# The diagonal ahead of the next chunk's first product, the ranks half a step later, and half of the row-rest moves on SyncE

## The chip, the cores and the metric

The kernel runs on one core of a Trainium2 chip. The metric is the time of one execution on the device in microseconds, the median over several runs. Engines are named as in the profile: PE is TensorE's matrix unit, DVE VectorE, ACT ScalarE, POOL GpSimd, and SP is SyncE, which here issues transfers (DMAs) and does no arithmetic.

## The reference

Three layers, one after another. An attention layer with a running state is computed for 4 x 8 heads over 768 tokens; its output becomes 3072 rows of 384, which go through a gated layer and then through a layer of 8 experts, of which each row takes one.

```python
state = np.zeros((B, H, D, D))
for t in range(S):
    kt, vt, rt = k[:, :, t], v[:, :, t], r[:, :, t]
    cur = np.einsum('bhd,bhe->bhde', u[None] * kt, vt)
    y[:, :, t] = np.einsum('bhd,bhde->bhe', rt, state + cur)
    state = w[None, :, :, None] * state + np.einsum('bhd,bhe->bhde', kt, vt)
x = y.transpose(0, 2, 1, 3).reshape(B * S, H * D)
x = ((1 / (1 + np.exp(-(x @ w_gate)))) * (x @ w_val)) @ w_out
logits = normalized(x) @ normalized(expert_emb).T / tau
e = argmax(logits, axis=1)
out = softmax(logits)[e] * (np.maximum(x @ w1[e], 0) @ w2[e])
```

## The kernel before, in words

The tokens are cut into 24 chunks of 128 (six to a batch). A chunk's inputs come in one load of 1152 KB (`load_chunk`) into a tile `ld`, of which there are two buffers, or `ldr`, a third one for every third chunk (2, 5, 8 and on). `load_chunk(c + 3)` stands at the end of chunk c, so a load waits until the chunk three before has been used up.

What is done with a chunk c is cut into stages:

- `at_p` (stage -2): products that scale the loaded fields. From chunk 9 on POOL does all five: rT by its table (L540), kT by its table (L541), r by k (L542), r by u (L543), k by its table (L544). Before chunk 9 one product on DVE (L538) does the first two.
- `at_s1` (stage 1): DVE sums the r products to `sd` (L552), and `at_diag` writes the diagonal of the score tile `Am` from it, on POOL (L564; up to chunk 5 partly on ACT).
- stage 2, `native_mask`: the scores that PE has left in PSUM are copied into `Am` above the diagonal by two predicated copies on DVE (L591).
- stage 4 (`at_P`, `at_Y1`, `at_T`), stage 5 (`at_Y2` and the next chunk's scores, `native_A`) and stage 6 (`at_X`, `at_D`, `load_chunk(c + 3)`). All of them put PE products into two PSUM banks, named `a0` and `a1` by their tags (tiles `py`). `at_X` writes the chunk's output, split in two words, to `xt`, and for the fourth part of the dims to `xp3`; `at_D` moves that part with six small transfers of 32 KB each for two chunks (L688) into the last 16 of each 64 rows of `xt`. All six are issued by POOL.

The gated layer runs over groups g of two chunks; from group 2 on two groups together, in steps of a gate half (`pgate`, nine products of 128x512, then ACT's sigmoid), a value half (`pval`, nine, then DVE's product `sgw`, ACT's `gth`, DVE's `gtl`) and twelve products into `o`. `at_tick` is called after each half, so a half step is the unit in which chunk stages are dealt out between these products. When a group's last `o` is there, `route_pick` chooses the expert of each row; two ticks later `route_rank` counts the rows per expert: three small PE products into `pr` (L782 to L784), which takes the bank `a1`, then four small DVE operations (L786 to L791), then POOL scatters the rows to DRAM (L793, `xs`).

`at_tick` calls the chunk stages of the tick first and then, if no chunk is between its stages 4 and 2 of the next (`open_y` is empty), the ranks that are due. So a rank that fell due beside a stage 2 stood directly behind the mask in the program. `pr` and the scores that the mask reads share bank `a1`, so `pr` waits until the mask has been read out.

After the groups come the experts, whose weights are loaded and split while PE multiplies. The library orders instructions of one engine by its own estimate of when each is ready, unless `follow(ins, before)` pins two of them.

Of the kernel before, what the change touches and what calls it, by code (L numbers as in the profile page):

```python
# [8 lines left out]
F32 = mybir.dt.float32  # L9
# [28 lines left out]
EARLY = 9  # L38
# [21 lines left out]
def kernel(  # L60
# [14 lines left out]
    nc = tc.nc  # L75
# [223 lines left out]
    if True:  # L299
# [45 lines left out]
        wd = c1.tile([P, 4], F32, name="wd")  # L345
        nc.sync.dma_start(out=wd, in_=wdec)
        ld = {}

        def load_chunk(c):
            if c % 3 == 2:  # L350
                t = r2p.tile([P, 3072], F32, tag="r2", name="ldr")[:, 0:2304]
            else:
                t = ldp.tile([P, 2304], F32, tag="ld", name="ld")
            for a, b in ((0, 1024), (1024, 2304)) if c == 0 else ((0, 2304),):
                nc.sync.dma_start(out=t[:, a:b], in_=att[c][:, a:b])
            ld[c] = t

        load_chunk(0)
# [147 lines left out]
        xp3 = c1.tile([P, 2, 256], F32R, name="xp3")  # L506
# [23 lines left out]

        def at_p(c):
            rT, kT, kt, v, r = fields(ld[c])
            if c < EARLY:

                nc.gpsimd.tensor_tensor(r, r, kt, op=ALU.mult)
                nc.gpsimd.tensor_tensor(r, r, ubt, op=ALU.mult)
                rk = ld[c][:, 0:1024].rearrange("p (b a n) -> p b a n", b=2, a=4)
                nc.vector.tensor_tensor(rk, rk, tabs, op=ALU.mult)  # L538
            else:
                nc.gpsimd.tensor_tensor(rT, rT, tabR, op=ALU.mult)  # L540
                nc.gpsimd.tensor_tensor(kT, kT, tabK, op=ALU.mult)  # L541
                nc.gpsimd.tensor_tensor(r, r, kt, op=ALU.mult)  # L542
                nc.gpsimd.tensor_tensor(r, r, ubt, op=ALU.mult)  # L543
            nc.gpsimd.tensor_tensor(kt, kt, tabKt, op=ALU.mult)  # L544
# [11 lines left out]
        def at_diag(c):  # L556
            if c < 4 and c % 2 == 1:
                Am = xtp.tile([P, 3072], F32, tag="xt", name="Am1")[:, 0:512].rearrange("p (h n) -> p h n", h=8)
            else:
                Am = Am0  # L560
            ams[c] = Am
            n = ACT_HEADS[c] if c < len(ACT_HEADS) else 0
            if n < 8:
                nc.gpsimd.tensor_tensor(  # L564
                    Am[:, n:8], same.unsqueeze(1).to_broadcast([P, 8 - n, HALF]),
                    sd[c % 2][:, n:8].unsqueeze(2).to_broadcast([P, 8 - n, HALF]), op=ALU.mult,
                )
            for h in range(n):
                nc.scalar.activation(Am[:, h, :], same, AF.Copy, scale=sd[c % 2][:, h:h + 1])

# [112 lines left out]
        def at_D(c):  # L683
            x = xt[c // 4][:, :, :, (c % 4 - 1) * P:(c % 4 + 1) * P]
            if c % 2 == 1 and c >= PERM:
                for h in range(2):
                    for k in range(3):
                        nc.gpsimd.dma_start(  # L688
                            out=x[64 * h + 48:64 * h + 64, k], in_=xp3[64 * h + 16 * k:64 * h + 16 * k + 16]
                        )  # L690

        gts = {}
        last_lo = []
        po = {}
        open_y = []
        scores = {}
# [287 lines left out]
        def rank_due(n):  # L984
            for r in ranks:
                r[0] -= 1
            while ranks and ranks[0][0] <= n:
                route_rank(*ranks.pop(0)[1])
# [114 lines left out]
        tick = 0  # L1103

        def at_tick():
            for c, st in sorted(stages.get(tick, [])):
                at_stage(c, st)
            if not open_y:
                rank_due(0)

        for g, f, wide in steps:
            if wide == 2:
# [366 lines left out]
```

## Time and profile before

| | |
|---|---|
| median of 3 runs | 851.79 us (848.81 to 854.65) |
| profiled execution | 849.21 us, span of its instructions 847.4 us |
| PE busy | 807.7 us, 95% of the span |
| DVE, ACT, POOL busy | 411.9, 321.8 and 243.7 us |
| granted TensorE clock, mean | 0.979 of full speed |
| POOL's small moves (L688) | 60 instructions, 31.1 us |

PE is busy in nine tenths or more of nearly every fortieth of the span; the exceptions are the first, a few slices around 120 to 160 us, two near 280 and 375 us, and the end. Idle time on the other engines costs nothing by itself. A wait is put down to what came last before the waiting instruction could start. Times of rows are microseconds from the start of the span.

### The profile page before, as it was taken

What the parts mean: (1) busy time and instruction counts of PE and PEld (TensorE: products, weight loads), DVE (VectorE), ACT (ScalarE), POOL (GpSimd) and SP (SyncE); (2) the same over time, 40 slices, a digit from 0 to 9 for tenths busy, and PEclk for the clock granted to TensorE, in tenths of its full rate; (3) what the DMA queues carried; (4) which work ended last, traced back from release to release, by engine and by line L of the source; (5) the groups of instructions that cost most, each with busy time, mean ns of one, the idle gap of its engine ahead of it and who ended that gap; (6) DMA issues with size and microseconds to landing.
All of it is one profiled execution on the core that took longest, in us unless ns stands there. A gap on an engine that the chain in (4) does not pass through costs nothing.

```text
span 847.4 us, 16892 instructions
## 1 busy us (share of the span) xinstructions
PE 807.7 (95%) x6941; PEld 722.2 (85%) x6941; DVE 411.9 (49%) x912; ACT 321.8 (38%) x695; POOL 243.7 (29%) x298
## 2 busy tenths in 40 slices
PE   5999998899999899979999999999999999999994
PEld 4889998788888788868878888888999989899993
DVE  6998764533343333433443324434474555565630
ACT  4776733222232122312232224334454455465530
POOL 6621034843435434453433111100210110110211
PEclk8699999999999999999999999999999999999997
DMA  8667832331212112121211002520476556554301
GB/s 325 262 237 276 264 105 76 123 105 58 66 57 84 35 53 64 73 83 56 67 57 31 21 10 71 182 74 0 109 241 203 171 189 212 170 194 141 122 20 34
DMA packets 36003, 100.03 MB, mean 118 GB/s; under 512 B 4731, under 2 KB 19207, under 8 KB 32975
## 3 DMA queue, kind: packets, MB, share of 16 engines
q1 hardware_dynamic: 29311, 87.27, 30.4%
q0 software_dynamic: 6608, 11.61, 4.5%
q8 instruction: 56, 0.92, 0.4%
q14 instruction: 28, 0.23, 0.1%
HBM read 81.12 MB, written 16.25 MB: 115 GB/s over the span
## 4 chain that ended last, share of the span: by engine, by line
PE 75%; DMA 6%; issue 6%; POOL 4%; DVE 4%; ACT 2%; SPq 0%; POOLq 0%; ACTq 0%; DVEq 0%
PE o L750 15%; PE pval L705 14%; PE pgate L705 13%; PE ph L899 9%; PE y L1266 9%; PE pgv L705 4%; PE py L625 3%; DMA ldr<-in_att_dram 3%; PE py L605 2%; DMA wraw<-in_wex_dram 1%; DMA raw<-in_wgv_dram 1%; POOL out_dram L1309 1%; PE pt L1231 1%; POOL Am L564 1%; PE py L582 1%
## 5 line engine op out<-in xcount | busy, mean ns | idle before, releaser
L705 PE MATMUL pval<-xt,gv 128*128 128x512 f32 x540 | 137.4, 399 | 0.0
L705 PE MATMUL pgate<-xt,gv 128*128 128x512 f32 x540 | 134.7, 394 | 1.4 <-DMA xt<-xp 1.4
L750 PE MATMUL o<-wo,gth 128*128 128x392 f32 x480 | 127.0, 346 | 0.0
L705 PEld LDWEIGHTS pval<-xt,gv 128*128 128x128 f32 x540 | 101.1, 190 | 22.7
L705 PEld LDWEIGHTS pgate<-xt,gv 128*128 128x128 f32 x540 | 100.7, 188 | 19.7 <-ACT xt L677 1.5
L899 PE MATMUL ph<-xk,we 128*128 128x336 f32 (+7 forms) x576 | 116.3, 349 | 0.0
L899 PEld LDWEIGHTS ph<-xk,we 128*128 128x128 f32 x576 | 102.5, 188 | 5.7 <-issue 1.2
L718 DVE TENSOR_TENSOR sgw<-pval,sgw 128x512 f32<-128x512 f32 x60 | 41.4, 691 | 132.5 <-PE pval L705 129.1
L1266 PE MATMUL y<-we,ht 128*128 128x384 f32 (+2 forms) x528 | 102.1, 340 | 0.0
L720 ACT ACTIVATE gth<-sgw 128x512 fp32r<-128x512 f32 x60 | 37.9, 632 | 159.1 <-DVE sgw L718 159.1
L1266 PEld LDWEIGHTS y<-we,ht 128*128 128x128 f32 (+2 forms) x528 | 92.2, 186 | 1.0
L750 PEld LDWEIGHTS o<-wo,gth 128*128 128x128 f32 x480 | 86.6, 188 | 4.3
L714 ACT ACTIVATE sgw<-pgate 128x512 f32<-128x512 f32 x60 | 36.3, 605 | 141.8 <-PE pgate L705 141.8
L750 PE MATMUL o<-wo,gtl 128*128 128x392 f32 x240 | 81.6, 340 | 0.0
L1309 POOL DMA_INDIRECT out_dram<-yo,xrow x26 | 27.7, 1066 | 173.4 <-ACT yo L1306 161.6
L722 DVE TENSOR_TENSOR gtl<-sgw,gth 128x512 fp32r<-128x512 f32 x60 | 49.6, 826 | 37.2 <-ACT gth L720 37.2
L819 DVE TENSOR_TENSOR we<-wraw,we 128x768 fp32r<-128x768 f32 x64 | 61.0, 957 | 9.2 <-ACT we L816 8.0
L904 DVE SCALAR_TENSOR_TENSOR ht<-ph,ht 128x384 fp32r<-128x384 f32 (+2 forms) x56 | 31.8, 567 | 62.8 <-ACT ht L903 62.5
L903 ACT ACTIVATE ht<-ph 128x384 fp32r<-128x384 f32 (+2 forms) x56 | 28.1, 502 | 83.5 <-PE ph L899 83.2
L705 PE MATMUL pgv<-xt,gv 128*128 128x256 f32 x432 | 58.3, 288 | 0.0
L705 PEld LDWEIGHTS pgv<-xt,gv 128*128 128x128 f32 x432 | 55.6, 194 | 0.6 <-ACT xt L677 0.3
L793 POOL DMA_INDIRECT xs<-xr,pi x24 | 25.1, 1044 | 107.1 <-DVE tot L1145 57.8
(247 smaller groups left out, 1115.2 us busy)
## 6 DMA issues: line engine op xcount, KB each, us to landing
wraw<-in_wex_dram SPq DMA_DIRECT2D x64, 384.0 KB, 3.1
ld<-in_att_dram SPq DMA_DIRECT2D x15, 1152.0 KB, 6.4
raw<-in_wgv_dram SPq DMA_DIRECT2D x12, 768.0 KB, 10.0
ldr<-in_att_dram SPq DMA_DIRECT2D x8, 1152.0 KB, 5.4
w2f<-in_wex_dram SPq DMA_DIRECT2D x8, 768.0 KB, 7.5
xs<-zt SPq DMA_DIRECT2D x8, 750.0 KB, 8.5
raw<-in_wout_dram SPq DMA_DIRECT2D x6, 768.0 KB, 9.5
xrow<-xs SPq DMA_DIRECT2D x5, 600.0 KB, 6.0
```

The costliest lines, as they stand in the source:

```text
L705: nc.tensor.matmul(pg, a, x[:, k, b, :], start=(n == 0), stop=(n == 8))
L714: nc.scalar.activation(sg, p0, AF.Sigmoid)
L718: nc.vector.tensor_tensor(sg, p1, sg, op=ALU.mult)
L720: nc.scalar.activation(hi, sg, AF.Copy)
L722: q = nc.vector.tensor_tensor(lo, sg, hi, op=ALU.subtract)
L750: nc.tensor.matmul(po[g][t], gt[a][:, ts_], w[:, f % 2, b, :], start=(f == 0 and n == 0), stop=(f == NF - 1 and n == 2))
L819: nc.vector.tensor_tensor(w[:, 768:1536], r, w[:, 0:768], op=ALU.subtract)
L899: nc.tensor.matmul(ph, a, x[:, k, b, :], start=(n == 0), stop=(n == 8))
L903: q = nc.scalar.activation(ht[:, 0, :], ph, AF.Relu)
L904: nc.vector.scalar_tensor_tensor(ht[:, 1, :], ph, 0.0, ht[:, 0, :], op0=ALU.max, op1=ALU.subtract)
L1266: nc.tensor.matmul(yo[e, t], ht[:, a, :], b, start=(f == 0 and n == 0), stop=(f == XF - 1 and n == 2))
L1309: q = nc.gpsimd.indirect_dma_start(out=out, out_offset=bass.IndirectOffsetOnAxis(ap=xrow[e][t].bitcast(I32)[:, 393:394], axis=0), in_=o, i ...
```

## The change

Four things are edited. `at_p` becomes a wrapper: for chunks 10 to 23 the first POOL product of a chunk (the rT one) must stand behind the last diagonal that was written out before it. `at_tick` calls the ranks ahead of the chunk stages. Of the six moves of `at_D` the three for the upper half (h = 1) are issued by SP, with source and destination read as plain f32. And the first load that is issued after them is pinned behind the last of them on SP's queue. In the new file each quoted line has a higher number: L551 to L555 are the products, L575 is the diagonal, L603 the mask, L700 the moves, L797 to L799 `pr`.

```diff
@@ -345,6 +345,7 @@
         wd = c1.tile([P, 4], F32, name="wd")
         nc.sync.dma_start(out=wd, in_=wdec)
         ld = {}
+        moves = []
 
         def load_chunk(c):
             if c % 3 == 2:
@@ -352,7 +353,9 @@
             else:
                 t = ldp.tile([P, 2304], F32, tag="ld", name="ld")
             for a, b in ((0, 1024), (1024, 2304)) if c == 0 else ((0, 2304),):
-                nc.sync.dma_start(out=t[:, a:b], in_=att[c][:, a:b])
+                q = nc.sync.dma_start(out=t[:, a:b], in_=att[c][:, a:b])
+                if moves:
+                    follow(getattr(q, "ins", q), moves.pop())
             ld[c] = t
 
         load_chunk(0)
@@ -530,6 +533,14 @@
 
         def at_p(c):
             rT, kT, kt, v, r = fields(ld[c])
+            first = len(nc.cur_bb.bb.instructions)
+            at_products(c)
+            if c > EARLY:
+                q = next(q for q in nc.cur_bb.bb.instructions[first:] if q.engine == mybir.EngineType.Pool)
+                follow(q, last_diag[-1])
+
+        def at_products(c):
+            rT, kT, kt, v, r = fields(ld[c])
             if c < EARLY:
 
                 nc.gpsimd.tensor_tensor(r, r, kt, op=ALU.mult)
@@ -561,10 +572,11 @@
             ams[c] = Am
             n = ACT_HEADS[c] if c < len(ACT_HEADS) else 0
             if n < 8:
-                nc.gpsimd.tensor_tensor(
+                q = nc.gpsimd.tensor_tensor(
                     Am[:, n:8], same.unsqueeze(1).to_broadcast([P, 8 - n, HALF]),
                     sd[c % 2][:, n:8].unsqueeze(2).to_broadcast([P, 8 - n, HALF]), op=ALU.mult,
                 )
+                last_diag[:] = [getattr(q, "ins", q)]
             for h in range(n):
                 nc.scalar.activation(Am[:, h, :], same, AF.Copy, scale=sd[c % 2][:, h:h + 1])
 
@@ -685,12 +697,15 @@
             if c % 2 == 1 and c >= PERM:
                 for h in range(2):
                     for k in range(3):
-                        nc.gpsimd.dma_start(
-                            out=x[64 * h + 48:64 * h + 64, k], in_=xp3[64 * h + 16 * k:64 * h + 16 * k + 16]
+                        q = (nc.sync if h else nc.gpsimd).dma_start(
+                            out=x[64 * h + 48:64 * h + 64, k].bitcast(F32),
+                            in_=xp3[64 * h + 16 * k:64 * h + 16 * k + 16].bitcast(F32),
                         )
+                moves[:] = [getattr(q, "ins", q)]
 
         gts = {}
         last_lo = []
+        last_diag = []
         po = {}
         open_y = []
         scores = {}
@@ -1103,10 +1118,10 @@
         tick = 0
 
         def at_tick():
+            if not open_y:
+                rank_due(0)
             for c, st in sorted(stages.get(tick, [])):
                 at_stage(c, st)
-            if not open_y:
-                rank_due(0)
 
         for g, f, wide in steps:
             if wide == 2:
```

What the library makes of it, at three places. The first is POOL around the products of chunk 16 (tile `ld_3294`), behind the moves of chunk 13. `Am` is the diagonal of chunk 14, `ld_3064` is chunk 15. Before:

```order
L688 DMA xt_3057<-xp3_197 16x2x256 x6
L540 TENSOR_TENSOR ld_3294<-ld_3294,tabs_174 128x512
L541 TENSOR_TENSOR ld_3294<-ld_3294,tabs_174 128x512
L542 TENSOR_TENSOR ld_3294<-ld_3294 128x384
L543 TENSOR_TENSOR ld_3294<-ld_3294,ubt_133 128x384
L544 TENSOR_TENSOR ld_3294<-ld_3294,tabKt_184 128x384
L564 TENSOR_TENSOR Am_192<-near_78,sd_196 128x512
L793 DMA xs_69<-xr_3028,pi_3350 3840x400 x2
```

After:

```order
L700 DMA xt_3057<-xp3_197 16x2x256 x3
L552 TENSOR_TENSOR ld_3294<-ld_3294,tabs_174 128x512
L575 TENSOR_TENSOR Am_192<-near_78,sd_196 128x512
L551 TENSOR_TENSOR ld_3064<-ld_3064,tabs_174 128x512
L553 TENSOR_TENSOR ld_3294<-ld_3294 128x384
L554 TENSOR_TENSOR ld_3294<-ld_3294,ubt_133 128x384
L555 TENSOR_TENSOR ld_3294<-ld_3294,tabKt_184 128x384
L808 DMA xs_69<-xr_3028,pi_3365 3840x400 x2
```

Of chunk 16 only the kT product is still ahead of chunk 14's diagonal, instead of all five; the rT product of chunk 15 comes right behind it. All even chunks from 12 to 22 show this order; at the odd chunks from 13 on four products are still ahead, and the rT one is behind.

In the same part of the program, PE around the rank of group 3 (`pr`), which falls due beside the mask of chunk 14. Before:

```order
L705 MATMUL pgate<-xt,gv 128x512 x9
L782 LDWEIGHTS ones
L782 MATMUL pr<-cum_96,ones 128x16
L783 LDWEIGHTS U
L783 MATMUL pr<-oh,U 128x16
L784 LDWEIGHTS ones
L784 MATMUL pr<-oh,ones 128x8
L705 MATMUL pval<-xt,gv 128x512 x9
L750 MATMUL o_3083<-wo,gth 128x392 x2
```

After:

```order
L720 MATMUL pgate<-xt,gv 128x512 x9
L720 MATMUL pval<-xt,gv 128x512 x9
L797 LDWEIGHTS ones
L797 MATMUL pr<-cum_96,ones 128x16
L798 LDWEIGHTS U
L798 MATMUL pr<-oh,U 128x16
L799 LDWEIGHTS ones
L799 MATMUL pr<-oh,ones 128x8
L765 MATMUL o_3083<-wo,gth 128x392 x2
```

The three `pr` products moved behind the value half. The ranks of groups 5 and 7 move in the same way.

The second place is PE around the rank of group 2, which fell due beside the mask of chunk 13. Before:

```order
L705 MATMUL pval<-xt,gv 128x512 x9
L782 LDWEIGHTS ones
L782 MATMUL pr<-cum_98,ones 128x16
L783 LDWEIGHTS U
L783 MATMUL pr<-oh,U 128x16
L784 LDWEIGHTS ones
L784 MATMUL pr<-oh,ones 128x8
L750 MATMUL o_3083<-wo,gth 128x392 x2
```

After:

```order
L720 MATMUL pgate<-xt,gv 128x512 x9
L797 LDWEIGHTS ones
L797 MATMUL pr<-cum_98,ones 128x16
L798 LDWEIGHTS U
L798 MATMUL pr<-oh,U 128x16
L799 LDWEIGHTS ones
L799 MATMUL pr<-oh,ones 128x8
L617 MATMUL py_3174<-ld 64x48 x7
L617 MATMUL py_3175<-ld 64x48 x8
```

It moved by twelve `o` products and a gate half, to a place directly ahead of the products `py` of chunk 13's stage 4, the second of which goes to the bank that `pr` holds. The ranks of groups 4 and 6, and of 0 and 1 as a pair, move like this one. The ranks of groups 8 to 11 stay.

The third place is DVE at chunk 8 (tile `ldr_1690`), the last whose first two products are done there, between gate operations (`sg`, `gt`) of group 1. Before:

```order
L538 TENSOR_TENSOR ldr_1690<-ldr_1690,tabs_174 128x1024
L735 TENSOR_TENSOR sg_1672<-pgv_1653,sg_1672 128x256
L738 TENSOR_TENSOR gt_1675<-sg_1672,gt_1675 128x256
L735 TENSOR_TENSOR sg_1711<-pgv_1692,sg_1711 128x256
L738 TENSOR_TENSOR gt_1714<-sg_1711,gt_1714 128x256
L552 TENSOR_REDUCE sd_196<-ld_806 128x8
L762 TENSOR_REDUCE rs_1735<-xr_1731 128x2
L764 TENSOR_TENSOR rs_1735<-xr_1731,rs_1735 128x16
L591 COPY_PREDICATED Am_192<-near_78,py0_1577 128x4x64
```

After:

```order
L750 TENSOR_TENSOR sg_1672<-pgv_1653,sg_1672 128x256
L753 TENSOR_TENSOR gt_1675<-sg_1672,gt_1675 128x256
L750 TENSOR_TENSOR sg_1711<-pgv_1692,sg_1711 128x256
L753 TENSOR_TENSOR gt_1714<-sg_1711,gt_1714 128x256
L563 TENSOR_REDUCE sd_196<-ld_806 128x8
L549 TENSOR_TENSOR ldr_1690<-ldr_1690,tabs_174 128x1024
L777 TENSOR_REDUCE rs_1735<-xr_1731 128x2
L603 COPY_PREDICATED Am_192<-near_78,py0_1577 128x4x64
L779 TENSOR_TENSOR rs_1735<-xr_1731,rs_1735 128x16
```

The product that waits for chunk 8's load stood ahead of two gate pairs and of chunk 6's `sd`; now it stands behind them, ahead of chunk 6's masks. On POOL chunk 6's diagonal is now ahead of chunk 8's products, not behind them. Nothing is changed on any engine before this place.

## Rows read from the trace of the kernel before

**Rows 1.** the waits of PE over the span: total us, times, longest us
```profile
PE pr L782 <- DVE Am L591: 9.5, 4, 4.7
...
PE o L750 <- ACT gt L737: 2.0, 1, 2.0
...
PE pgate L705 <- DMA xt<-xp: 1.4, 1, 1.4
```

**Rows 2.** PE's timeline, 255 to 300 us: start, us, operation, [idle before]
```profile
283.70 0.18 PE L782 MATMUL pr<-cum,ones 128*128 128x16 bf16 x1 [2.94 <-DVE Am L591]
...
283.77 0.17 PE L784 MATMUL pr<-oh,ones 128*128 128x8 bf16 x1
283.79 2.30 PE L705 MATMUL pval<-xt,gv 128*128 128x512 f32 x9
```

**Rows 3.** PE's timeline, 366 to 384 us
```profile
367.96 2.23 PE L705 MATMUL pgate<-xt,gv 128*128 128x512 f32 x9
374.85 0.19 PE L782 MATMUL pr<-cum,ones 128*128 128x16 bf16 x1 [4.66 <-DVE Am L591]
...
374.94 3.75 PE L705 MATMUL pval<-xt,gv 128*128 128x512 f32 x9
```

**Rows 4.** PE's timeline, 425 to 472 us
```profile
444.34 0.17 PE L782 MATMUL pr<-cum,ones 128*128 128x16 bf16 x1 [1.37 <-DVE Am L591]
```

**Rows 5.** the stretch 374 to 380 us: busy us, then PEclk, DMA share, GB/s
```profile
374.00:380.00 6.00, 5.16 (x21) 4.40 (x22) 2.15 (x7) 0.47 (x1) 2.10 (x2) 0.72 0.19 68
```

**Rows 6.** POOL's timeline, 255 to 300 us
```profile
271.78 3.10 POOL L688 DMA_DIRECT2D xt<-xp  x6 [2.95 <-DVE xp L676]
275.83 1.29 POOL L540 TENSOR_TENSOR ld<-ld,tabs 128x512 f32<-128x512 f32 x1 [0.95 <-DMA ld<-in_att_dram]
...
281.80 1.04 POOL L564 TENSOR_TENSOR Am<-near,sd 128x512 f32<-128x512 f32 x1
```

**Rows 7.** POOL's timeline, 300 to 600 us
```profile
367.01 1.29 POOL L540 TENSOR_TENSOR ldr<-ldr,tabs 128x512 f32<-128x512 f32 x1 [2.70 <-DMA ldr<-in_att_dram]
368.26 1.74 POOL L541 TENSOR_TENSOR ldr<-ldr,tabs 128x512 f32<-128x512 f32 x1
...
372.94 1.04 POOL L564 TENSOR_TENSOR Am<-near,sd 128x512 f32<-128x512 f32 x1
```

**Rows 8.** DVE's timeline, 255 to 300 us
```profile
271.83 0.29 DVE L680 TENSOR_TENSOR xt<-py,xt 128x128 fp32r<-128x128 f32 x1 [0.35 <-ACT xt L679]
...
278.85 0.54 DVE L552 TENSOR_REDUCE sd<-ldr 128x8 f32<-128x384 f32 x1
282.87 0.77 DVE L591 COPY_PREDICATED Am<-near,py 128x256 f32<-128x256 uint32 x2 [3.48 <-POOL Am L564]
283.97 0.17 DVE L786 TENSOR_TENSOR rs<-pr,slot 128x16 f32<-128x16 f32 x1 [0.32 <-PE pr L784]
```

**Rows 9.** the chain that ended last, in order of time: start us, us, what
```profile
123.13 7.72 DMA ldr<-in_att_dram
...
155.71 4.43 DMA xt<-xp
...
269.73 5.96 DMA ld<-in_att_dram
...
359.15 7.72 DMA ldr<-in_att_dram
```

**Rows 10.** timeline of SyncE's queue, 355 to 365 us
```profile
359.15 0.33 SPq L355 DMA_DIRECT2D ldr<-in_att_dram  x1
```

**Rows 11.** DVE's timeline, 345 to 384 us
```profile
361.25 0.29 DVE L680 TENSOR_TENSOR xt<-py,xt 128x128 fp32r<-128x128 f32 x1 [0.35 <-ACT xt L679]
```

**Rows 12.** DVE's timeline, 112 to 166 us
```profile
130.87 1.23 DVE L538 TENSOR_TENSOR ldr<-ldr,tabs 128x1024 f32<-128x1024 f32 x1 [5.66 <-DMA ldr<-in_att_dram]
```

**Rows 13.** PE's timeline, 112 to 166 us
```profile
132.94 1.44 PE L750 MATMUL o<-wo,gt 128*128 128x392 f32 x6 [1.96 <-ACT gt L737]
...
137.59 0.68 PE L605 MATMUL py<-ld 64*64 64x48 f32 x32
```

## The prediction

> **What bounds the kernel now.** I read the page's busy shares first, then PE's waits, then the timelines around the longest of them, then the chain that ended last. PE is busy nearly all the time, so a shift of work pays only where PE itself stands still. Among the waits of PE three belong to things that this change touches: `pr` on DVE's mask, 9.5 us in four times; an `o` product on ACT's `gt`, 2.0 us; the first `pgate` of the wide steps on the moves into `xt`, 1.4 us [rows 1]. That is 12.9 us, the whole stake but for the clock.
>
> The long stalls have one shape. A chunk's load is issued, POOL's next products wait for it, five of them run, then the diagonal of the chunk two before, then the mask, then `pr`, and PE's value half is queued behind `pr`. At chunk 16: load issued at 269.73, 5.96 us [rows 9]; products from 275.83, diagonal at 281.80 to 282.84 [rows 6]; mask to 283.64 [rows 8]; `pr` at 283.70 after 2.94 us of idle PE [rows 2]. At chunk 20: load at 359.15, 7.72 us [rows 9]; products from 367.01, diagonal at 372.94 [rows 7]; `pr` at 374.85 after 4.66 us [rows 3]. The third is 1.37 us at 444.34 [rows 4], and the fourth must be 9.5 less these three, 0.5 us.
>
> [...]
>
> **The change part by part.** *SyncE's three moves and the load behind them.* The last of the moves needs the last piece of `xt`, which DVE writes at 271.83 for 0.29 us [rows 8]. I price a move on SyncE by the only duration seen on that queue near here, a load's 0.33 us [rows 10]; the other end is what POOL takes, 3.10 us for six, 0.52 each [rows 6]. Two moves can go before that piece is ready, so chunk 16's load is issued at 272.12 + 0.33 = 272.45 at best, 2.7 us later than before, and some 1.2 us later still if all three queue up behind the piece at POOL's price. At chunk 20 the piece is ready at 361.54 [rows 11] and the load goes at 361.9, also 2.7 us later. The same 2.7 us serve for chunk 8. The loads of odd chunks have no moves ahead of them and keep their time. This is the cost side of the edit: SyncE's queue holds the load behind moves that wait for DVE, and POOL's products wait for the load.
>
> *The diagonal ahead.* At even chunks the path from landing to mask loses four of five products. Before, landing (275.69) to the end of the mask (283.64) was 7.95 us; what stays is 0.14 us to start, one product of 1.29, the diagonal's 1.04 and the mask's 0.77 [rows 6, 8], with hand-overs 3.3 us. Chunk 14's `sd` ends at 279.39 [rows 8] and doesn't hold it. So at chunk 16 the mask ends at 272.45 + 5.96 + 3.3 = 281.7, and 284.7 with the slowest issue and the longer load of 7.72. At chunk 20 it ends at 361.9 + 7.72 + 3.4 = 373.0; 371.2 with the shorter load, 374.6 with everything at its worst, POOL's product at 1.74 [rows 7] among it.
>
> *The rank half a step later.* The value half goes ahead of `pr`, about 2.2 us [rows 3]. PE ran dry at 283.70 - 2.94 = 280.76, so `pr` comes at 283.0 at chunk 16, with the mask there since 281.7: the stall is gone, 2.94 us. At chunk 20 PE ran dry at 370.19, `pr` comes at 372.4, the mask is there at 373.0: 0.6 of 4.66 us stays (0 to 2.2). The 1.37 us go whole, since that rank moves by a gate half and twelve `o` products and chunk 21's diagonal has an unmoved load; the 0.5 us likewise, by the half step alone. Together 9.5 - 0.6 = 8.9 us. [...]
>
> What the later rank costs: at groups 2, 4 and 6 `pr` now stands directly ahead of the chunk's first products, and the second half of these needs the bank that DVE has yet to read. From the last `pr` product's start to the end of DVE's read is 284.14 - 283.77 = 0.37 us [rows 2, 8]; seven small products on the other bank cover about a third. I take 0.25 us for each of groups 2 and 6, 0.4 for the pair of groups 0 and 1, nothing at group 4, where other products stand between: 0.9 us. The bounds are 0 and five times the whole way from the first `pr`, 0.44 us, 2.2 us. The scatter comes later too: POOL queues it ahead of the next moves, which slip by some 0.3 us at the odd places; the load is later than that, so it is covered.
>
> *Chunk 8.* DVE's product for chunk 8 waited 5.66 us for the load [rows 12] with two gate pairs queued behind, which cost PE 1.96 us at `o` [rows 13]. With the pairs ahead of it that wait goes. What is late next is chunk 6's mask, now behind that product: the load lands at 123.13 + 2.7 + 7.72 = 133.55, the product takes 1.23 [rows 12], a small operation and the mask 1.0, so 135.8. PE needs it just after its products that began at 137.59 [rows 13], now 1.96 earlier, 135.6, and these run 0.7 us before the first that reads the mask. It fits with 0.5 us to spare: 2.0 us gained, 0 if the load is 2.5 us later than I think.
>
> *The first wide step.* `pgate` waited 1.4 us for the last of POOL's six moves, 4.43 us from issue to landing [rows 1, 9]. With three on each queue POOL saves three times 0.52 us, but the last piece of `xt` still sets when the last move can go. I take 1.0 us, bounds 0 and 1.4.
>
> *Sum.* 8.9 + 1.5 + 2.0 + 1.0 - 0.9 = 12.5 us less. With all bounds at their best 14.4; with all at their worst 9.5 - 3.9 - 2.2 = 3.4, where 3.9 is 1.7 left at chunk 16 and 2.2 at chunk 20. Against the profiled execution's 849.21 us that is 836.7; against the median of the runs, 851.79, which is 2.6 above it, 839.3. What comes after 600 us is queued behind PE's own order and moves up with it. The POOL products that now fall beside other DVE work may lengthen each other, as the 1.74 us beside 1.29 hints [rows 7]; the most that this adds to a mask is 0.45 us. [...]
>
> **The rivals.** *Half of it*: the loads land later than I take them, by 2 us each. Then chunk 16 keeps a stall of 0.7 us and chunk 20 one of 2.6, the clock's 1.5 us are not won, chunk 8 gives 0.5 and the first wide step its 1.0: 9.5 - 3.3 + 0.5 + 1.0 - 0.9 = 6.8 us, 845.0. For it: these loads vary between 5.96 and 7.72 us [rows 9]; against it: I took the longer one where it counts.
>
> *No change*: the half step only moves the wait to the bank's next user. If DVE's read of `pr` sits behind slower work than I see, each of five places costs 1 to 2 us, and with loads as late as in the rival above little is left: 849 to 852. Against it: in the order of the new kernel the DVE work ahead of that read belongs to a value half that PE has finished a gate half earlier.
>
> *Slower*: the load isn't carried beside the moves but only after they have landed, or SyncE issues them late. A move's issue to landing was 4.43 us [rows 9]. With that on top, chunk 16's mask ends at 286.1 against `pr` at 283.0, 3.1 us; chunk 20's at 377.4 against 372.4, 5.0 us with the clock loss of 1.5; chunk 8's mask comes at 140.2 against 136.3, 3.9 us: 13.5 us of stalls for the 2.94 + 4.66 + 1.5 + 2.0 = 11.1 that stood there. With 1.37 and 0.5 gained, 0.9 paid and nothing at the first wide step it ends at +1.4. From there every further microsecond costs three, so it decides at loads some 7 us later than I forecast: 860 and up. Against it: the moves are 32 KB against 1152, and nothing else is in flight on SyncE's queue there. [...]
>
> **How the numbers follow.** About 1% is what a measurement of this kernel can tell from no change; that is 843.3 and 860.3 here. The forecast has 0.6 and runs from 836 to 843. Half of it has 0.22 and ends within 1% more often than not; no change 0.13; slower 0.05. So faster 0.63, same 0.32, slower 0.05. The range leaves out 2 in 10: from 835, the best bound of 837.4 less part of the 3 us by which the runs before lie about their median, to 848, which takes in half of it and the worst bounds, 3.4 us less than before. The likeliest is 839.3.
>
> **What the profile of the changed kernel would show.** PE's waits without `pr` on the mask, or at one place under 1 us; no `o` on `gt` near 131 us; new waits of a few tenths of `py` (L617) on DVE's `rs` at groups 0, 2 and 6; no stretch at a clock of 0.72 near 370. Even loads issued 2.7 us later against PE's work, behind three moves; diagonals 1 to 3 us earlier all the same. It would be wrong if SyncE's moves took several microseconds of the queue, if loads grew past 8 us, or if PE's idle time came back at `pr` or `py` in the same amount.

## The result and the profile after

The changed kernel takes 840.07 us, median of 6 runs (838.75 to 842.65), beside 850.38 us for the kernel before (848.17 to 854.65, 6 runs). The ratio is 0.9876, with a 95% interval of 0.9854 to 0.9897. The profiled executions are 838.75 and 849.21 us, so 10.5 us apart, where the sum had 12.5. The total came out near the forecast, but its terms did not: the later ranks cost several times what they were priced at, and other terms made up for most of it.

PE's waits over the span in the profile after, in the columns of [rows 1]:

```profile
PE py L637 <- issue: 1.8, 4, 0.7
...
PE py L617 <- DVE Am L603: 1.0, 2, 0.5
...
PE pr L797 <- DVE Am L603: 0.2, 1, 0.2
```

The 9.5 us of `pr` on the mask [rows 1] are 0.2 us. The waits of `o` on ACT's `gt` and of `pgate` on the moves have no row left. Of the waits behind the start of the program the one that has grown most is on `issue`, time in which PE waited for nothing that the profile shows: 0.8 us in one wait before.

PE's timeline after at chunk 16 and at chunk 20, the places of [rows 2, 3]:

```profile
279.03 2.23 PE L720 MATMUL pgate<-xt,gv 128*128 128x512 f32 x9
281.09 2.20 PE L720 MATMUL pval<-xt,gv 128*128 128x512 f32 x9
283.14 0.18 PE L797 MATMUL pr<-cum,ones 128*128 128x16 bf16 x1
...
366.62 2.23 PE L720 MATMUL pgate<-xt,gv 128*128 128x512 f32 x9
368.68 2.20 PE L720 MATMUL pval<-xt,gv 128*128 128x512 f32 x9
371.05 0.18 PE L797 MATMUL pr<-cum,ones 128*128 128x16 bf16 x1 [0.17 <-DVE Am L603]
```

At chunk 16 `pr` doesn't wait; at chunk 20 it waits 0.17 us. The nine value products there take 2.20 us, not 3.75 [rows 3]. The stretch after that answers to [rows 5], in the same columns:

```profile
366.00:374.00 8.00, 7.83 (x41) 6.67 (x40) 4.84 (x10) 1.33 (x3) 6.03 (x6) 1.00 0.04 14
```

The clock is 1.00. Of the stretch of [rows 5], before, a part had a clock of 0.50 and the end 1.00 again:

```profile
375.00:378.00 3.00, 3.00 (x10) 2.40 (x8) 0.69 (x4) 0.00 (x0) 1.49 (x2) 0.50 0.06 24
379.00:380.00 1.00, 1.00 (x8) 1.00 (x7) 0.49 (x1) 0.47 (x1) 0.00 (x0) 1.00 0.61 205
```

So the 1.5 us of the sum, the value half's 3.75 less the gate half's 2.23 [rows 3], are back.

POOL's timeline after at chunks 16 and 20, for [rows 6, 7]:

```profile
271.95 1.62 POOL L700 DMA_DIRECT2D xt<-xp  x3 [0.45 <-DVE xp L688]
279.18 1.28 POOL L552 TENSOR_TENSOR ld<-ld,tabs 128x512 f32<-128x512 f32 x1 [5.62 <-DMA ld<-in_att_dram]
280.43 1.04 POOL L575 TENSOR_TENSOR Am<-near,sd 128x512 f32<-128x512 f32 x1
...
367.89 1.29 POOL L552 TENSOR_TENSOR ldr<-ldr,tabs 128x512 f32<-128x512 f32 x1 [4.83 <-DMA ldr<-in_att_dram]
369.13 1.05 POOL L575 TENSOR_TENSOR Am<-near,sd 128x512 f32<-128x512 f32 x1
```

One product stands ahead of the diagonal instead of five. SyncE's queue after, for [rows 10], and the loads of chunks 8 and 20 in the chain that ended last, for [rows 9]:

```profile
359.34 1.93 SPq L700 DMA_DIRECT2D xt<-xp  x3
361.38 0.51 SPq L356 DMA_DIRECT2D ldr<-in_att_dram  x1
```

```profile
126.58 5.57 DMA ldr<-in_att_dram
361.38 6.37 DMA ldr<-in_att_dram
```

Three moves hold SyncE's queue for 1.93 us, 0.64 each. The load behind them lands in 5.57 and 6.37 us, where the same two took 7.72 without moves ahead of them [rows 9].

**Where the time went.** The gate halves (the first `pgate` of each wide step) are the same sixty in every kernel here, so a kernel can be laid beside the kernel before by the difference of their starts. In microseconds, start in the kernel named minus start before; a negative number in a stretch is time gained there:

| stretch, by the time before | what lies in it | after | even ranks back | no half step | no pin on products |
|---|---|---|---|---|---|
| up to 171.0 | start, chunk 8, first wide step | -3.36 | -2.51 | -2.17 | +0.20 |
| 171.0 to 186.5 | ranks of groups 0 and 1 | +3.17 | +1.01 | 0.00 | +1.27 |
| 256.9 to 272.3 | rank of group 2 | +0.68 | +0.18 | 0.00 | +0.28 |
| 278.5 to 288.1 | chunk 16, rank of group 3 | -3.11 | -3.10 | -1.96 | -3.10 |
| 288.1 to 296.9 | behind it | +0.62 | +0.04 | -0.01 | -0.01 |
| 346.2 to 361.7 | rank of group 4 | +0.67 | -0.11 | -0.11 | +0.41 |
| 368.0 to 380.7 | chunk 20, rank of group 5 | -5.96 | -6.29 | -5.32 | -5.79 |
| 380.7 to 389.3 | behind it | +0.27 | +0.22 | 0.00 | -0.01 |
| 438.6 to 455.5 | chunk 22, rank of group 6 | -0.83 | -1.34 | +0.03 | -1.24 |
| 461.7 to 468.8 | rank of group 7 | -0.68 | -0.68 | +0.02 | -0.69 |
| last gate half, 581.5 | all of these | -8.54 | -12.60 | -9.53 | -8.67 |

After that another 0.35 us are won up to PE's last product, and the rest, 1.5 us, lies behind the last scatter of the output (below).

One thing limits the row of groups 0 and 1. The trace of the kernel before, from which all these differences are taken, has POOL's scatters from 177.23 to 182.38 us beside the same products, and PE doesn't pause there:

```profile
179.79 0.68 PE L605 MATMUL py<-ld 64*64 64x48 f32 x32
180.29 0.43 PE L625 MATMUL py<-Am,ld 64*64 64x64 f32 x16
```

In the changed kernel, and in some of the others, PE does pause beside these scatters (next section). What a kernel loses here by such pauses alone can't be put on its later ranks.

### The profile page after: what moved, and what is told of

The parts are those of the page before. It is cut to its first block, busy times and chain, and to the rows that moved or that the text cites. A ratio compares the mean times of both kernels' runs of the same rounds, so it can differ in the third digit from the quotient of the medians.

```text
span 837.0 us, 16946 instructions
## 1 busy us (share of the span) xinstructions
PE 810.4 (97%) x6941; PEld 725.3 (87%) x6941; DVE 411.0 (49%) x912; ACT 322.2 (38%) x695; POOL 225.6 (27%) x268
## 4 chain that ended last, share of the span: by engine, by line
PE 75%; issue 12%; DVE 4%; DMA 3%; POOL 2%; ACT 2%; SPq 0%; POOLq 0%; DVEq 0%; ACTq 0%
PE o L765 17%; PE pval L720 15%; PE pgate L720 14%; PE y L1281 7%; PE ph L914 7%; PE py L637 4%; PE pgv L720 4%; POOL out_dram L1324 2%; PE py L617 2%; DMA ldr<-in_att_dram 1%; DMA raw<-in_wgv_dram 1%; PE py L594 1%; PE pt L1246 1%; PE ph L1354 1%; PE y L1305 1%
## 5 line engine op out<-in xcount | busy, mean ns | idle before, releaser
L834 DVE TENSOR_TENSOR we<-wraw,we 128x768 fp32r<-128x768 f32 x64 | 61.0, 957 | 11.4 <-ACT we L831 9.4
L737 DVE TENSOR_TENSOR gtl<-sgw,gth 128x512 fp32r<-128x512 f32 x60 | 44.1, 735 | 37.9 <-ACT gth L735 37.2
L831 ACT ACTIVATE we<-wraw 128x768 fp32r<-128x768 f32 x64 | 53.3, 838 | 8.7 <-DMA wraw<-in_wex_dram 4.8
## 6 DMA issues: line engine op xcount, KB each, us to landing
raw<-in_wout_dram SPq DMA_DIRECT2D x6, 768.0 KB, 12.5
```

Of the source, the lines that this page charges most:

```text
L737: q = nc.vector.tensor_tensor(lo, sg, hi, op=ALU.subtract)
L831: q = nc.scalar.activation(w[:, 0:768], r, AF.Copy)
L834: nc.vector.tensor_tensor(w[:, 768:1536], r, w[:, 0:768], op=ALU.subtract)
```

## The experiments

Each set of runs has the kernel before beside it, and the ratio is to that. Intervals are 95%. Four rows of the table make a set: the first four, the next four and the last four. Each set ran on a chip of its own, so a difference between sets can be one between chips. Line numbers in the profile rows are each kernel's own.

| kernel | median us | before, same set | ratio |
|---|---|---|---|
| even ranks back | 837.07 | 852.25 | 0.9845 (0.9806 to 0.9884) |
| scatters later | 841.41 | 852.25 | 0.9897 (0.9856 to 0.9938) |
| half step alone | 847.97 | 852.25 | 0.9961 (0.9933 to 0.9989) |
| no moves on SyncE | 843.35 | 852.25 | 0.9921 (0.9894 to 0.9948) |
| no half step | 837.48 | 849.70 | 0.9851 (0.9805 to 0.9896) |
| moves and load alone | 844.01 | 849.70 | 0.9915 (0.9886 to 0.9943) |
| no pin on products | 838.11 | 849.70 | 0.9859 (0.9819 to 0.9900) |
| even back, pair's scatters later | 835.96 | 849.70 | 0.9825 (0.9785 to 0.9866) |
| changed kernel again | 842.12 | 852.53 | 0.9877 (0.9853 to 0.9902) |
| even ranks back again | 835.90 | 852.53 | 0.9808 (0.9783 to 0.9833) |
| pin on products alone | 846.08 | 852.53 | 0.9926 (0.9899 to 0.9953) |
| even back, pair's scatters later, again | 835.08 | 852.53 | 0.9796 (0.9770 to 0.9823) |

**Even ranks back.** Only the ranks of groups 3, 5 and 7 keep the half step:

```diff
             while ranks and ranks[0][0] <= n:
-                route_rank(*ranks.pop(0)[1])
+                r = ranks.pop(0)[1]
+                if r[0] in (3, 5, 7):
+                    waiting.append(r)
+                else:
+                    route_rank(*r)
...
             if not open_y:
-                rank_due(0)
+                while waiting:
+                    route_rank(*waiting.pop(0))
             for c, st in sorted(stages.get(tick, [])):
                 at_stage(c, st)
+            if not open_y:
+                rank_due(0)
```

> The changed kernel, with the ranks of groups 0, 1, 2, 4 and 6 put back to their place in the kernel before (directly behind the masks, ahead of twelve o products) and only those of groups 3, 5 and 7 half a step later. In the trace of the changed kernel PE falls back against its own steps at four places, by 3.2 us between the gate halves of the pair of groups 0 and 1 and by 0.85, 0.90 and 0.86 us at groups 2, 4 and 6, 5.8 us in all, and each time it is the stretch behind a later rank. Theory 'place': it is the later rank with what hangs on it (pr, DVE's read, the scatter) that costs this; then this kernel gets 5.0 to 5.8 us less than the changed one, about 834.5 against 840.1, and no pr wait on a mask comes back beyond 0.5 us. Rival 'elsewhere': these losses come from the loads, the moves or the diagonal, which stay as they are; then the time is within 1 us of the changed kernel. Rival 'the even ranks needed it too': pr waits on a mask again at groups 2, 4 and 6, and the time is 1 to 4 us more.

The ratio was 0.9845. In the table of stretches 2.2 of 3.2 us came back at the pair and 0.5 to 0.8 at each of groups 2, 4 and 6; no wait of `pr` on a mask is left. So the late even ranks bought nothing and cost time, as theory "place" has it, but less than its 5.0 to 5.8 us: 4.1 by the traces at the last gate half, 3.0 by the medians, with intervals that overlap. The profiled execution of this kernel gained less before 171 us than the changed kernel's did (-2.51, not -3.36), and the granted clock differs there; the stretch 156 to 162 us of this run, then of the changed kernel, in the columns of [rows 5]:

```profile
156.00:162.00 6.00, 6.00 (x68) 5.02 (x61) 0.92 (x3) 1.43 (x4) 2.14 (x2) 0.73 0.92 368
```

```profile
156.00:162.00 6.00, 6.00 (x97) 5.14 (x93) 1.63 (x6) 1.43 (x4) 1.58 (x2) 1.00 0.98 341
```

The clock is 0.73 in the one and 1.00 in the other. Of the eight other kernels and repeats with moves on SyncE four had a lower clock in this stretch too (0.56 to 0.74), and none of the kernels without them (1.00 in all four). What lowers it was not found: PE had been busy for 5.29 of the 6 us before, and in the changed kernel for 5.28.

At chunk 11 a pause remained, in PE's timeline of the same run:

```profile
177.78 0.75 PE L637 MATMUL py<-Am,ld 64*64 64x64 f32 x14
178.91 0.27 PE L637 MATMUL py<-Am,ld 64*64 64x64 f32 x2 [0.38 <-issue]
```

Sixteen such products take 0.43 us elsewhere. POOL issued the pair's scatters from 174.72 to 179.85.

**Scatters later.** This looks at those pauses. In the changed kernel, PE's timeline at the pair:

```profile
180.78 1.05 PE L637 MATMUL py<-ld,T 48*64 48x64 f32 x32
181.78 0.37 PE L637 MATMUL py<-Am,ld 64*64 64x64 f32 x4
182.54 0.36 PE L637 MATMUL py<-Am,ld 64*64 64x64 f32 x6 [0.39 <-issue]
183.29 0.36 PE L637 MATMUL py<-Am,ld 64*64 64x64 f32 x6 [0.39 <-issue]
```

```diff
-            for t in range(2):
-                q = nc.gpsimd.indirect_dma_start(
+            def scatter():
+                for t in range(2):
+                    q = nc.gpsimd.indirect_dma_start(
...
+            if g in (0, 1, 2, 4, 6):
+                held.append(scatter)
```

`at_D` then calls what is held, behind its moves.

> The changed kernel, with the scatters of groups 0, 1, 2, 4 and 6 on POOL behind the next moves instead of ahead of them, some 3 to 8 us later; pr and DVE's read of it stay at the later place. Theory 'scatter in flight': PE's short products of stage 5 stand still for 0.3 to 0.5 us at a time, with no releaser, while the scatters of the later rank are on their way (269.5, 357.2 and 444.3 us, and twice at 182 to 183.4), and DVE's T at chunk 11 starts 1.6 us after its products; then 2.5 to 4 of the 5.8 us come back and the stage 5 products behind these ranks take 0.41 us for sixteen again, about 837 us. Theory 'bank': the loss is that pr stands directly ahead of py, whose second half waits for DVE's read of the bank, and splits the value half; then 0 to 1 us comes back, about 839.5. If the scatters only take their stalls with them to where they are now, the large gate and value products there show none, since theirs are few per us.

At the pair it did what the theory says; PE's timeline of this run:

```profile
183.75 0.69 PE L637 MATMUL py<-ld,T 48*64 48x64 f32 x32
184.26 0.41 PE L637 MATMUL py<-Am,ld 64*64 64x64 f32 x16
```

The stretch cost 1.22 us, not 3.17, and at the four places together (the pair and groups 2, 4 and 6) 3.0 of 5.4 us came back. But the ratio, 0.9897, did not fall. One reason is a new wait that the edit brought on POOL, ahead of chunk 16's product:

```profile
281.91 0.11 POOL L791 MEMSET xr<- 128x12 f32 x1 [4.82 <-DMA xs<-xr,pi]
```

A scatter issued beside the load landed late, the memset of `xr` waited 4.82 us for it, the diagonal came late, and `pr` waited again, 1.36 us at chunk 16 and 1.29 at chunk 20:

```profile
PE pr L803 <- DVE Am L603: 2.6, 2, 1.4
```

The other reason has nothing to do with the scatters: up to 171.0 us, ahead of the first one that is moved, this trace has gained 0.40 us where the changed kernel's has 3.36, and its clock in the stretch 156 to 162 us is 0.72. So the ratio alone decides neither theory; the stretches speak for "scatter in flight".

**Half step alone, and no moves on SyncE.** The first is the kernel before with the new `at_tick`; the second the changed kernel with the old six lines of moves and the old load.

```diff
         def at_tick():
+            if not open_y:
+                rank_due(0)
             for c, st in sorted(stages.get(tick, [])):
                 at_stage(c, st)
-            if not open_y:
-                rank_due(0)
```

> The kernel before, with only the ranks half a step later; products, diagonals, moves and loads as they were. Theory 'three parts': the rank alone keeps 2.2 us of cover at chunks 16 and 20 and all at chunk 22, so the pr waits fall from 9.5 to 0.7 + 2.4 = 3.1 us, part of the clock's 1.5 us comes back, the 5.8 us of the later even ranks are paid, chunk 8's 2.0 us wait and the first wide step's 1.4 us stay: 6.4 + 1.0 - 5.8, so 1 to 2 us less than before, about 849. Rival 'the rank does it': the saving of the whole change is the rank's, about 840. Rival 'loss belongs to the moves': the even ranks cost nothing here, about 843.

```diff
-                        q = (nc.sync if h else nc.gpsimd).dma_start(
+                        nc.gpsimd.dma_start(
...
-                if moves:
-                    follow(getattr(q, "ins", q), moves.pop())
```

> The changed kernel without its part on SyncE: all six moves by POOL as before, and the next load free of them; the diagonal ahead and the later rank stay. Theory 'the moves carry the early gains': chunk 8's wait at o (2.3 us gained, 0.9 given back a little later) and the first wide step's wait (1.7 us gained) come back, and so 3 us are lost; at chunks 16 and 20 the loads are earlier by some 2 us and no wait of pr comes back; 843. Rival 'they cost': the earlier loads are worth more than what the moves give, 838 to 840. Rival 'they carry the change': the stalls at chunks 16 and 20 come back as well, 848.

The half step alone has a ratio of 0.9961, some 3 to 4 us; `pr` waited 2.8 us in two places, against 3.1 expected, and the losses behind the later even ranks were there in full (3.18, 0.65 and 0.62 us at the first three): theory "three parts". Without the moves on SyncE the time is the expected 843, but not for that reason alone. Its waits of PE on the mask:

```profile
PE pr L793 <- DVE Am L601: 2.1, 1, 2.1
```

A wait at chunk 20 came back. In that kernel's order four products stand ahead of chunk 18's diagonal again, although the pin on the products is there. From chunk 12 on, in all kernels here, the diagonal of an even chunk stands behind a single product where the load is pinned behind moves, and behind four or five where it isn't: the library seems to put the diagonal early only where it reckons the load to be late.

**No half step; moves and load alone; no pin on products.** The three edits take the halves of the change apart: the old `at_tick`; the old `at_tick` and no pin; no pin.

```diff
-            if c > EARLY:
-                q = next(q for q in nc.cur_bb.bb.instructions[first:] if q.engine == mybir.EngineType.Pool)
-                follow(q, last_diag[-1])
```

> The changed kernel with all ranks at their place in the kernel before; the moves, the load behind them and the diagonal ahead stay. Worked from the run with only the even ranks put back, where PE's gate half at chunk 20 ends at 365.6 us and the mask at 367.2, and at chunk 16 at 279.3 and about 280.6: a rank directly behind these gate halves waits 1.6 and 1.3 us there, and the old 1.4 and 0.5 us of chunk 22 and behind come back. Theory 'both are needed': 4.5 us more than with the even ranks put back, about 841.5, the same as the changed kernel by another way. Rival 'the diagonal is enough': no more than 1 us above that run, 837 to 838, and pr waits below 1 us in all. Rival 'the rank carries it': 846 or more.

> The kernel before with only three of the six moves on SyncE and the next load pinned behind them. The order of instructions that comes out of it has chunk 14's diagonal behind a single product of chunk 16 and chunk 18's behind a single one of chunk 20, as in the changed kernel, though nothing pins products behind the diagonal: it is the later load that makes the library put it ahead. Theory 'the pinned load carries the diagonal': the time is that of the kernel without the half step, within 1 us, about 841.5. Rival 'the products behind the diagonal carry it': pr waits of 2.9 and 4.7 us stay as they were, and only the 2.5 to 3.4 us at chunk 8 and at the first wide step are won, about 848.

> The changed kernel without the pin of a chunk's first product behind the last diagonal; moves, pinned load and half step stay. At even chunks the order keeps the diagonal behind one product. Theory 'the pin is worth nothing': within 1 us of the changed kernel, about 840. Rival 'the pin carries the diagonal': pr waits of 1.2 and 1.5 us at chunks 16 and 20 as with the rank alone, and 3 to 5 us more, about 844.

The waits of PE on the mask, without the half step and then with moves and load alone:

```profile
PE pr L797 <- DVE Am L603: 3.7, 4, 1.4
```

```profile
PE pr L794 <- DVE Am L600: 6.6, 5, 2.5
```

Without the half step 0.96 and 0.79 us of the 2.94 and 4.66 [rows 2, 3] remained at chunks 16 and 20, and the old 1.4 and 0.5 us; the ratio is 0.9851, as good as the changed kernel's 0.9876. "Both are needed" falls: the half step is worth at most those 3.7 us of waits, and gives back 2.5 to 4.4 (below). The time is that of the rival "the diagonal is enough", though not its waits of below 1 us. The 1.4 us, at group 6, isn't the half step's alone: chunk 23's load took 7.9 us from issue to POOL's first product there, and with the even ranks back, where that rank stands at the same place, it took 5.9 and `pr` did not wait. With moves and load alone the waits at chunks 16 and 20 are 0.84 and 1.18 us, so the load that is pinned late does carry the diagonal of even chunks. What neither theory had is 1.49 us at group 2 and 2.53 at group 6, where the mask is an odd chunk's: without the pin all five products stand ahead of an odd chunk's diagonal, with it four. Neither theory's time came out either: 844.01 us lies 6.5 above the kernel without the half step and 4 below the 848 of the rival, and 2.7 of the 6.5 lie up to 171.0 us, where this trace has a clock of 0.56 in the stretch 156 to 162 us. With the half step the same pin is worth nothing measurable (0.9859 without it).

**The pair's scatters later, with the even ranks back.** The edit for the scatters, for groups 0 and 1 alone, on top of the even ranks back.

> The run with only the even ranks put back, and the four scatters of groups 0 and 1 issued by POOL behind chunk 11's moves instead of beside its stage 4. With the even ranks put back PE still lost 1.0 us there against the kernel before: the sixteen Am products beside the scatters took 0.75 us and then stood still for 0.38. Theory 'scatter in flight': this 0.8 to 1.0 us comes back, about 836 us, and those products take 0.43 us again with no wait. Rival 'it moves on': the scatters slow the products or a load where they are now, and the time stays at 837.

The ratio was 0.9825 and the pair cost nothing. But no kernel of this set paused beside a scatter, with the scatters beside the same products or not, so it could not tell. PE's timeline of the kernel without the pin, whose scatters start 1.57 us behind the first `pr` like those of the changed kernel:

```profile
184.34 0.69 PE L634 MATMUL py<-ld,T 48*64 48x64 f32 x32
184.86 0.41 PE L634 MATMUL py<-Am,ld 64*64 64x64 f32 x16
```

**All in one set, and the pin alone.** So the changed kernel and the two best ones ran once more together, with the kernel before plus only the pin.

> The changed kernel once more, beside the three others here. In the traces so far PE's short products paused for 0.3 to 0.4 us beside a scatter in the changed kernel and in the four kernels of the first set (with the even ranks back, with the scatters later, with the rank alone, without the moves on SyncE), and in none of the four of the second set, though the one without the pin has its ranks and scatters at the very same times against PE's work. Theory 'kernel': the pauses belong to the later rank with its scatter; then they are here again, 3.5 us are lost at the pair of groups 0 and 1 and 5.8 at the four places, and the time is 3 us above that with the even ranks back. Rival 'where it runs': they belong to the chip or the execution and not to the kernel; then all four kernels of this set have them or none has, and if none, the pair loses 1.6 us and the four places 2.8 us, as without the pin, and the time is 1 to 2 us above that with the even ranks back.

> The kernel with the even ranks put back, once more, in the same set as the changed kernel. Theory 'kernel': 3 us below the changed kernel, and PE's products of chunk 11 pause again beside the scatters, 1.0 us. Rival 'where it runs': pauses here only if the changed kernel has them too; 1 to 2 us below it if it has none. Rival 'no difference': the later even ranks cost nothing that a median can tell, within 1 us.

> The kernel before with only the pin of a chunk's first product behind the last diagonal. In its order four of the five products are still ahead of the diagonals of chunks 14 and 18, and only the rT product stands behind, since the load is where it was. Theory 'the pinned load carries the diagonal': only that one product's 1.25 us is taken off the way to the mask, at chunks 16 and 20, with part of the clock's 1.5 us: 1.5 to 3 us less than before. Rival 'the pin carries it': the stalls of 2.9 and 4.7 us shrink to 1 us or less, 6 us or more below before.

> The even ranks put back and the scatters of groups 0 and 1 behind chunk 11's moves, once more, in the same set. Theory 'kernel': 1 us below the run with the even ranks back, which pauses at chunk 11 where this one does not. Rival 'where it runs': within 0.5 us of it, since neither or both pause.

In this set the pauses were back in every kernel that has scatters beside these products: 3.29 us lost at the pair in the changed kernel, 1.07 with the even ranks back, and 1.13 with the pin alone, whose ranks stand where they stood before. PE's timeline with the pin alone, at the products that took 0.43 us without a pause in the trace before:

```profile
180.67 0.84 PE L635 MATMUL py<-Am,ld 64*64 64x64 f32 x15
181.91 0.21 PE L635 MATMUL py<-Am,ld 64*64 64x64 f32 x1 [0.41 <-issue]
```

With the pair's scatters moved away the stretch cost 0.00; PE's timeline there:

```profile
177.05 0.68 PE L617 MATMUL py<-ld 64*64 64x48 f32 x32
177.55 0.43 PE L637 MATMUL py<-Am,ld 64*64 64x64 f32 x16
```

So both answers hold a part: whether PE pauses beside a scatter differs from one set of runs to another, and where it does, the place of the scatter decides what it costs. The even ranks back are 6.2 us below the changed kernel in the same set (0.9808 against 0.9877, with intervals apart); the two traces account for 3.7 of that at the last gate half, and the changed kernel's trace is the fastest of its six executions. The scatters of the pair give another 0.8 by the medians, inside the intervals. At 835.08 us this has the lowest median. The pin alone won 6.4 us by the medians, more than its theory's 1.5 to 3 and as much as the rival "the pin carries it" asked for, but its waits are not the rival's:

```profile
PE pr L793 <- DVE Am L601: 4.9, 3, 3.2
```

1.15 and 3.23 us were left at chunks 16 and 20, and the 1.37 us of [rows 4] were gone, so the one product behind the diagonal is worth more than its own 1.25 us, but it doesn't carry the stalls.

## Why the prediction was right, and where it wasn't

The forecast of 839.3 was 0.8 us from the median, and part of that is luck. The sum had 12.5 us less, and 10.3 were measured by the medians; it was taken off a median of 851.79, which over six runs is 850.38. The terms err in both directions.

- **The waits of `pr` and the clock, 8.9 + 1.5.** Right, and a little small: 3.11, 5.96, 1.69 and 0.68 us, 11.4 together (the 1.69 is the changed kernel's gain from 438.61 to 446.64, by the same gate halves). The 1.5 of the sum is 3.75 less 2.23 us [rows 3]; after, the nine value products took 2.20. That the stall is what lowers the clock was an estimate, and the runs show no more than this: behind 4.66 us of idle PE the clock was 0.50 for 3 us, without them it is 1.00, and behind 2.94 us, at chunk 16, the value half took 2.30 us [rows 2]. The mask at chunk 20 left 0.17 us where 0.6 was forecast. The 0.45 us that work of POOL and DVE side by side might have added to a mask were not put to the test there: DVE was idle for 2.93 us ahead of that mask, so nothing of its work lay beside the product and the diagonal, which took 1.29 and 1.05 us:

```profile
370.22 0.78 DVE L603 COPY_PREDICATED Am<-near,py 128x256 f32<-128x256 uint32 x2 [2.93 <-POOL Am L575]
```

- **What the later rank costs, 0.9 us.** This is the step that failed. Against the trace before, the four places took 3.17, 0.68, 0.67 and 0.86 us, 5.4 in all, beyond the stated bound of 2.2 (the 0.86 is group 6's, behind the 1.69 above); the stretches behind the ranks of groups 3 and 5 took 0.62 and 0.27 more, 6.3 altogether. Not all of the 5.4 is the later place, since PE paused in this trace and not in the one before: kernels with these ranks at their old place lose 1.0 to 1.1 us at the pair and up to 0.2 at each of groups 2 and 6 in the sets that pause. Within one set the later place costs 4.0 to 4.4 us at the four places where PE pauses, and 2.5 where it doesn't (1.27, 0.28, 0.52 and 0.45). The mechanism named, the bank's next user waiting for DVE's read, fits what is left without pauses at groups 2, 4 and 6. At the pair the value half was cut into one and eight products around the second half of `py`, which the prediction did not price. Of the waits of `py` on `rs` that it expected to see, the profile shows none that the kernel before doesn't have. What is more than that goes with PE's pauses beside the scatters; of the later scatter the prediction had priced only the moves that queue behind it.
- **Chunk 8, 2.0 us.** 2.33 us were gained at `o`, and 0.94 given back behind it, where `py` waited 0.52 us for chunk 6's mask and 0.85 for `T`; 1.4 net. What was called next, that mask, had no 0.5 us to spare: DVE's product took 2.03 us, not 1.23 [rows 12]:

```profile
132.17 2.03 DVE L549 TENSOR_TENSOR ldr<-ldr,tabs 128x1024 f32<-128x1024 f32 x1 [0.24 <-DMA ldr<-in_att_dram]
```

- **The first wide step, 1.0 us.** 1.66 us here, but only 0.1 to 0.3 in four of the five runs whose clock falls at 156 to 162 us, and a loss of 1.3 in the fifth.
- **SyncE's moves.** 0.64 us each, not 0.33, so chunk 16's load left at 273.73 instead of 272.45, 0.8 us late after allowing for 0.5 us by which PE was late there. The cover was enough. The loads did not suffer behind the moves: 5.57 and 6.37 us, against 7.72 without them [rows 9].
- **Not in the sum:** 1.5 us behind the last scatter, 0.35 before it, and 0.3 at the start.

The rivals: "half of it" had the loads 2 us later than taken; chunk 16's first product began at 279.18 us where the forecast's terms give 278.6, and chunk 20's at 367.89 where they give 369.8. "Slower" had loads that suffer; they did not. "No change" had the right place and size, 1 to 2 us at five places behind a later `pr`, where 5.4 at four was measured, and was outweighed; its mechanism, slow work of DVE ahead of the read, is not what the runs show.

The attribution was off as well. By the prediction's own times a rank left at its place would have waited 0.9 us at chunk 16 and 2.8 at chunk 20, and 1.37 and 0.5 behind them. Without the half step 0.96, 0.79, 1.41 and 0.52 us were measured, and the ratio is 0.9851: chunk 20's stall goes by the pinned load with the pin on the products, and what the half step took off elsewhere it gave back. By the stretches it is worth its price at groups 3, 5 and 7 alone; by the medians of the second set, keeping it there, with the pair's scatters later, gains 1.5 us over leaving it out, inside the intervals.

## What to carry to other kernels

When a step is moved by a rule that catches all its instances, price each instance: here three of eight ranks gained by the half step and the other five paid for it. Follow the whole of what a moved step issues, its scatters too, into the work that it then lies beside. And where a scheduler orders by its own estimate, pinning one transfer can reorder another engine; the order has to be read for each part of a change alone, or the gain goes to the wrong part.

## What the runs showed that I had not expected

**Pauses beside a scatter.** In the changed kernel and in the kernels of the first and third set that have scatters there, PE's 64x64 products stood still for 0.29 to 0.46 us at a time while POOL's scatters were under way, and DVE's `T` at chunk 11 began 1.6 us after its products had ended in the changed kernel. They don't seem to be the loading of instructions. The DMA queues of the changed kernel in 178 to 184 us, where it pauses (packets, MB, share):

```profile
q0 software_dynamic: 256, 0.82, 36.6%
```

Its queue of instructions over the whole span:

```profile
q8 instruction: 56, 0.92, 0.4%
```

In the stretch only the scatters' queue moved anything; the nearest packets of q8 lie at 177.5 to 178 and 184.5 to 185. What makes PE pause, and why it never did in the second set or in the trace of the kernel before, stays open. The sets ran on different chips; on which ones the two executions of the part above ran is not on record. The traces differ in one more thing: the profile holds 5874 to 6074 updates of semaphores for the changed kernel and the first and third set, and 6490 to 6510 for the second set and the kernel before. Whether the chip or the recording has to do with the pauses was not tried.

**The end of the program.** The last scatter of the output begins at 835.90 us of 847.4 before, and at 827.02 of 837.0 after:

```profile
835.90 1.30 POOL L1309 DMA_INDIRECT out_dram<-yo,xrow  x1 [2.90 <-ACT yo L1306]
```

```profile
827.02 1.30 POOL L1324 DMA_INDIRECT out_dram<-yo,xrow  x1 [2.90 <-ACT yo L1321]
```

That is 11.5 and 10.0 us. In all traces of kernels with six moves by POOL it is 11.5, and in all with three on SyncE 9.8 to 10.0, with nothing else changed there: 30 transfers fewer on POOL's queue go with 1.5 us less at the end. Why was not tried.
